# The main part of a Fourier and gated two-layer kernel in 31 chunks instead of 34, with fourth-stage units that may lie across two chunks

## The chip, the cores and the metric

The kernel runs on one core of a Trainium2 chip. Its metric is the device time of one execution in microseconds; the smaller, the better. Engines are named as in the profile: PE (matrix products, with PEld for its weight loads), DVE, ACT and POOL (elementwise work), SP (issues transfers).

## The reference, cut to what matters

```python
X = np.fft.rfft(x, axis=1)                    # x: 8 x 3008 x 256
F = (filt_r + 1j * filt_i)[None, :, :]
y = np.fft.irfft(X * F, n=3008, axis=1)       # 24064 tokens of 256
h = y.reshape(24064, 256) @ w_in              # 256 x 2048
g = h * np.cos(h)
out = g @ w_out                               # 2048 x 256
```

All of it is fp32. The kernel splits each operand of a product into a high and a low part and makes three matmuls of one product (high with high, low with high, high with low).

## The kernel before

The transform is computed as matrix products in four stages, one batch of 3008 tokens after the other. Stage 1 (L351 to L361) makes one matmul of 96 x 512 at L357, which DVE copies out of PSUM at L359. Stages 2 and 3 (L364 to L415) are made of triples of matmuls of 512 columns at L280 to L282. Behind a stage-2 triple DVE multiplies by the filter in six instructions: four at L398, one at L399, one at L400, and the last of them frees the PSUM buffer. ACT frees that of stage 3 by the copy at L413. Stage 4 (L521 to L581) works in units of 235 tokens: a load, four or eight short matmuls of 120 columns at L547, a copy of ACT at L572, two operations of DVE at L573 and L574, and the split into a high part (ACT, L577) and a low part (POOL, L578), which land in the y tiles of a chunk. All four stages share two PSUM buffers, which the program calls ps.

The y tiles feed the main part, which takes the first 15604 tokens in 34 chunks: 32 of 470 tokens and two of 282. A chunk has eight steps. In each, `hidden` (L676) makes 12 matmuls of the chunk's width into one of two PSUM buffers called hp (L684). `gate` (L692) then goes over twice the width in each instruction: ACT rounds (L694), DVE subtracts (L695), ACT takes the sine (L698), DVE multiplies (L699) and with this frees hp, ACT casts to gh (L704), POOL makes the remainder gl (L705). Two steps later, `project` (L709) makes 12 matmuls (L719) of gh and gl into the two accumulators acc0 and acc1, of which there is one each. After the eighth step ACT copies each of them into a tile o (L731), which frees it for the next chunk, and issues the store (L732). The tiles o come from a pool of their own with two buffers. Each chunk's tokens are two whole stage-4 units, so that a unit never crosses a chunk's end. After the main part a tail, which is not touched, takes the other 8460 tokens in wide blocks.

Work of the transform is planned into the main part's steps by a table of due times (`plan` and `run_due`, L977 to L998); the step at which the fourth-stage unit of a chunk falls due is counted back from that chunk's begin (`BEFORE4`, `EACH4`). The list scheduler of the framework then sets each engine's order. An engine works its queue in that order; the numbers behind names, as in hp_9813, are the program's own running numbers and differ between the two programs.

Of the kernel before, what the change touches and what calls it, by code (L numbers as in the profile page):

```python
# [10 lines left out]
F32 = mybir.dt.float32  # L11
# [8 lines left out]
NK = 24  # L20
# [17 lines left out]
BEFORE4, EACH4 = 68, 12  # L38
SMALL, FAST = 4, 34
HALF = 252  # L40
# [137 lines left out]
def fft_filter_then_cos_glu(ctx: ExitStack, tc: tile.TileContext, ins, outT):  # L178
# [29 lines left out]
    def load_mats(*names):  # L208
        for i, name in enumerate(names):
# [6 lines left out]
            m = const.tile([rows, 2 * cols], F32R, name=name)  # L216
# [3 lines left out]
    def load_full(*names):  # L220
        for name in names:
            mats[name] = const.tile(list(ins[name].shape), F32, name=name)
            nc.sync.dma_start(mats[name], ins[name])
# [7 lines left out]
    chunks = _chunks()  # L231
    RUN = 5 * TJ
    token0 = chunks[FAST][0] * TJ
# [224 lines left out]
    z2c = dram.tile([4, chunks[0][1], n23 - DIRECT, 2 * D], F32, name="z2c", bufs=1)  # L458
# [11 lines left out]
    def first23(i, fas, fbs):  # L470
# [38 lines left out]
        if i < n23 - DIRECT:  # L509
            nc.sync.dma_start(z2c.rearrange("e g i c -> (e g) i c")[:, i], z[: 4 * chunks[0][1]])  # L510
# [11 lines left out]
    def stage4(c, half):  # L522


        j0, n = chunks[c]
        r, w = n * NK, n * Q
        rows = z2.rearrange("j q d -> (j q) d")[j0 * 2 * Q + half * w :][:w]
        zf = fft.tile([P, 2, D], F32, name="z4", tag="ld", bufs=5)[:r]
        if c == 0:
            zf = zf[: 10 * (n23 - DIRECT)]  # L530
            of = z2c[2 * half : 2 * half + 2].rearrange("a g i (k d) -> (g i k) a d", k=2)
# [634 lines left out]
```

## Time and profile before

| | us |
|---|---|
| median of three runs | 2420.87 |
| fastest and slowest run | 2420.4, 2420.91 |
| profiled execution | 2419.05 |
| its span | 2417.2 |
| PE busy | 2386.4 |
| POOL busy | 1822.7 |
| ACT busy | 1672.6 |
| DVE busy | 1647.6 |

The profiled execution lasts 1.85 us longer than its span, and it is 1.82 us faster than the median. Busy time of PE is the union of its matmuls' spans; a matmul's span reaches into the next one's, so the interval from start to start is what one costs in a row.

### The profile page before, as it was taken

What the parts mean: (1) busy time and instruction counts of PE and PEld (TensorE: products, weight loads), DVE (VectorE), ACT (ScalarE), POOL (GpSimd) and SP (SyncE); (2) the same over time, 40 slices, a digit from 0 to 9 for tenths busy, and PEclk for the clock granted to TensorE, in tenths of its full rate; (3) what the DMA queues carried; (4) which work ended last, traced back from release to release, by engine and by line L of the source; (5) the groups of instructions that cost most, each with busy time, mean ns of one, the idle gap of its engine ahead of it and who ended that gap; (6) DMA issues with size and microseconds to landing.
All of it is one profiled execution on the core that took longest, in us unless ns stands there. A gap on an engine that the chain in (4) does not pass through costs nothing.

```text
span 2417.2 us, 36437 instructions
## 1 busy us (share of the span) xinstructions
PE 2386.4 (99%) x12703; PEld 2091.1 (87%) x12703; DVE 1647.6 (68%) x2376; ACT 1672.6 (69%) x2521; POOL 1822.7 (75%) x1463
## 2 busy tenths in 40 slices
PE   7999999999999999999999999999999999999999
PEld 2788998888888888888888888888999999999998
DVE  5846756675576667667666766765777777777776
ACT  4876677667677766766776676666767677676776
POOL 3886678878697877879787887965777777777775
PEclk9999999999999999999999999999999999999999
DMA  8844354534464454445555453541000000000000
GB/s 294 251 158 131 126 141 129 185 127 133 127 199 151 136 185 140 140 140 172 157 145 173 142 151 102 187 148 48 22 22 30 22 26 26 22 26 26 22 14 18
DMA packets 188303, 277.62 MB, mean 115 GB/s; under 512 B 19440, under 2 KB 103344, under 8 KB 188120
## 3 DMA queue, kind: packets, MB, share of 16 engines
q1 hardware_dynamic: 155448, 223.11, 30.7%
q10 hardware_dynamic: 32672, 52.18, 6.0%
q8 instruction: 101, 1.65, 0.3%
q14 instruction: 82, 0.67, 0.1%
HBM read 177.16 MB, written 98.06 MB: 114 GB/s over the span
## 4 chain that ended last, share of the span: by engine, by line
PE 95%; DMA 2%; DVE 1%; ACT 0%; POOL 0%; SPq 0%; issue 0%; ACTq 0%; POOLq 0%; DVEq 0%
PE hp L684 28%; PE acc L719 28%; PE acc L849 15%; PE x L765 8%; PE w L765 4%; PE ps L547 4%; PE ps L765 2%; PE ps L357 2%; PE ps L280 2%; PE ps L281 2%; PE ps L282 2%; DMA zf<-z1f 1%; PE ps L330 0%; DMA xf<-in_x 0%; DMA raw<-in_w_out 0%; DMA ff<-in_fb 0%
## 5 line engine op out<-in xcount | busy, mean ns | idle before, releaser
L705 POOL TENSOR_TENSOR gl<-g,gh 128x940 fp32r<-128x940 f32 (+1 forms) x264 | 574.8, 2178 | 242.4 <-ACT gh L704 155.7
L684 PE MATMUL hp<-y,w_in 128*128 128x470 f32 (+1 forms) x3264 | 751.8, 373 | 5.3 <-DVE g L699 4.6
L684 PEld LDWEIGHTS hp<-y,w_in 128*128 128x128 f32 x3264 | 604.6, 189 | 92.2 <-issue 5.7
L719 PE MATMUL acc<-gh,w_out 128*128 128x470 f32 (+1 forms) x2176 | 608.6, 373 | 0.0
L719 PEld LDWEIGHTS acc<-gh,w_out 128*128 128x128 f32 x2176 | 404.5, 189 | 58.0 <-issue 1.7
L695 DVE TENSOR_TENSOR g<-g,hp 128x940 f32<-128x940 int32 (+1 forms) x272 | 301.3, 1108 | 187.9 <-ACT g L694 181.7
L699 DVE TENSOR_TENSOR g<-g,hp 128x940 f32<-128x940 f32 (+1 forms) x272 | 301.5, 1108 | 165.4 <-ACT g L698 163.2
L698 ACT ACTIVATE g<-g,half_pi 128x940 f32<-128x940 f32 (+1 forms) x272 | 289.8, 1065 | 136.7 <-DVE g L695 134.1
L719 PE MATMUL acc<-gl,w_out 128*128 128x470 f32 (+1 forms) x1088 | 373.1, 375 | 0.8 <-POOL gl L705 0.8
L704 ACT CAST gh<-g 128x940 fp32r<-128x940 f32 (+1 forms) x272 | 260.7, 958 | 116.4 <-DVE g L699 108.6
L694 ACT ACTIVATE g<-hp 128x940 int32<-128x940 f32 (+1 forms) x272 | 254.5, 936 | 114.4 <-PE hp L684 111.0
L352 POOL TENSOR_TENSOR xh<-xf,xh 48x512 fp32r<-48x512 f32 x192 | 245.5, 1291 | 34.2 <-ACT xh L351 23.2
L747 ACT ACTIVATE qg<-qg,half_pi 128x496 f32<-128x496 f32 (+1 forms) x272 | 188.2, 712 | 77.4 <-DVE qg L746 77.4
L719 PEld LDWEIGHTS acc<-gl,w_out 128*128 128x128 f32 x1088 | 204.2, 188 | 30.4 <-POOL gl L705 1.4
L359 DVE COPY z1t<-ps 96x512 f32<-96x512 f32 x192 | 130.5, 685 | 113.3 <-PE ps L357 111.2
L398 DVE SCALAR_TENSOR_TENSOR sw<-ps,sg,f 64x256 f32<-64x256 f32 x336 | 162.5, 483 | 51.0 <-PE ps L282 46.0
L849 PE MATMUL acc<-hg,w_out 128*128 128x496 f32 (+1 forms) x548 | 185.0, 392 | 0.0
L849 PE MATMUL acc<-hgh,w_out 128*128 128x496 f32 (+1 forms) x544 | 183.5, 391 | 0.6 <-POOL hgh L827 0.6
L849 PE MATMUL acc<-hgl,w_out 128*128 128x496 f32 (+1 forms) x540 | 182.4, 392 | 0.0
L351 ACT CAST xh<-xf 96x512 fp32r<-96x512 f32 x192 | 114.3, 616 | 26.8 <-PE ps L357 26.1
L404 POOL TENSOR_TENSOR yl<-ya,yh 128x512 fp32r<-128x512 f32 x84 | 108.9, 1298 | 27.2 <-ACT yh L403 19.5
L771 ACT COPY sum<-x 128x496 f32<-128x496 f32 (+1 forms) x136 | 78.5, 577 | 58.6 <-PE x L765 58.2
(163 smaller groups left out, 4190.1 us busy)
## 6 DMA issues: line engine op xcount, KB each, us to landing
xf<-in_x SPq DMA_DIRECT2D x224, 192.0 KB
z<-z1t SPq DMA_DIRECT2D x192, 192.0 KB
z<-z SPq DMA_DIRECT2D x98, 240.0 KB
f<-in_fb SPq DMA_DIRECT2D x84, 256.0 KB
f<-in_fa SPq DMA_DIRECT2D x84, 256.0 KB
zf<-z SPq DMA_DIRECT2D x84, 256.0 KB
z<-z2t ACTq DMA_DIRECT2D x84, 256.0 KB
zg<-z SPq DMA_DIRECT2D x72, 256.0 KB
```

The lines of the kernel that those rows point to most:

```text
L352: nc.gpsimd.tensor_tensor(xh[:Q], xf[:Q, v], xh[:Q].bitcast(F32), ALU.subtract)
L684: mm = nc.tensor.matmul(hp[:, u, :nt], w_in[s][w][:, t, fs], y[:, t, :nt], start=(t == 0 and n == 0), stop=(t == NDT - 1 and n == 2))
L694: rounded = nc.scalar.activation(g.bitcast(I32), h, AF.Copy, bias=0.25)
L695: rest = nc.vector.tensor_tensor(g, g.bitcast(I32), h, ALU.subtract)
L698: sine = nc.scalar.activation(g, g, AF.Sin, bias=half_pi, scale=-TWO_PI)
L699: mult = nc.vector.tensor_tensor(g, g, h, ALU.mult)
L704: cast = nc.scalar.copy(gh, g)
L705: lower = engine.tensor_tensor(gl, g, gh.bitcast(F32), ALU.subtract)
L719: nc.tensor.matmul(acc, w_out[s][w][:, u, es], g[:, u], start=(s == 0 and u == 0 and n == 0), stop=(s == NFT // 2 - 1 and u == 1 and n == 2))
L747: nc.scalar.activation(g, g, AF.Sin, bias=half_pi, scale=-TWO_PI)
L765: nc.tensor.matmul(bank[:, p * n : (p + 1) * n], ws[a], y[b], start=first and p == i == 0, stop=last and i == 2, skip_group_check=True)
L849: nc.tensor.matmul(acc, w[a][:, u, e * P : (e + 1) * P], b[:, :, p], start=(q, u, p, n) == (0, 1, 0, 0), stop=(end and p == 1 and n == 2))
```

## The change

The main part takes the same 15604 tokens in 31 chunks: four of 470, one of 464 and 26 of 510 tokens. The stage-4 units keep their size, and 26 of them now lie across the begin of a chunk: such a unit goes to a tile y4s (one buffer), its split is made in two pieces, and the second piece is written when the next chunk has begun (`LATE4`). Its due times count from the begin of the chunk before (`APART4`, `EACH4`). The y tiles and the gate tiles are now laid out for 512 tokens, at multiples of 64 bytes in each row; before, a second half began at 1880 bytes. To make room, the pool of the o tiles is gone, and every o takes a buffer of a ring of five ("ld") that the transform's loaded tiles and their first sums use (zf, z4); and the constants of the start and of the main part share buffers. The diff, cut:

```diff
-BEFORE4, EACH4 = 68, 12
-SMALL, FAST = 4, 34
-HALF = 252
+HALF, WIDE = 252, 512
+SIZES = [470] * 4 + [464] + [510] * 26
+APART4, EACH4, LATE4 = 22, 10, 3
...
+def _units():
+    pairs = [5] * 8 + [3] * 4 + [5] * ((2 * B * NJ - 52) // 5)
+    starts = np.concatenate([[0], np.cumsum(pairs)])
+    return [(int(a), int(c), int(a) * NA) for a, c in zip(starts, pairs)]
...
-            m = const.tile([rows, 2 * cols], F32R, name=name)
+            m = const.tile([P, 2 * cols], F32R, name=name, tag=name)[:rows]
...
-        if c not in ys:
-            ys[c] = [ypool.tile([P, NDT, 5 * TJ], F32R, name=f"y{i}") for i in range(2)]
-        y = fft.tile([P, 2 * HALF], F32, name="y4", bufs=1)[:, : NDT * 5 * NA]...
+            parts = [(k, max(t0, begins[k]), min(t0 + size, begins[k + 1])) for k in range(len(SIZES)) if ...]
+            if len(parts) > 1:
+                flat = outs_pool.tile([P, NDT, 5 * NA], F32, name="y4s")
+            else:
+                flat = fft.tile([P, 512], F32, name="y4", bufs=1)[:, : NDT * 5 * NA]...
...
-        cast = nc.scalar.copy(yh, y)
-        sub = (nc.vector if c < 2 else nc.gpsimd).tensor_tensor(yl, y, yh.bitcast(F32), ALU.subtract)
+        for i, (k, a, b) in enumerate(parts):
+            if i:
+                yield
+            if k not in ys:
+                ys[k] = [ypool.tile([P, 1024], F32R, name=f"y{i}").rearrange("p (t n) -> p t n", t=NDT) for i in range(2)]
+            yh, yl = (v[:, :, a - begins[k] : b - begins[k]] for v in ys[k])
+            of = flat[:, :, a - t0 : b - t0]
+            cast = nc.scalar.copy(yh, of)
+            sub = (nc.vector if u < 4 else nc.gpsimd).tensor_tensor(yl, of, yh.bitcast(F32), ALU.subtract)
...
-        g = moe.tile([P, 2, HALF * 2], F32, name="g")[:, :, :nt]
+        g = moe.tile([P, 2, WIDE], F32, name="g")[:, :, :nt]
...
-                if stages:
-                    o = fft.tile([P, 512], F32, name="o", tag="ld", bufs=5)[:, :nt]
-                else:
-                    o = opool.tile([P, RUN], F32, name="o")[:, :nt]
+                o = fft.tile([P, 512], F32, name="o", tag="ld", bufs=5)[:, :nt]
...
+                at = [slot(begins[k - 1]) + 2 + (t0 - first) * APART4 / (5 * NA) + t * EACH4 for t in range(NDT)]
+            ready = lambda k=k, ready=ready: ready() and now_at[0] >= k - 1
+            if t0 + n * NA > begins[k + 1]:
+                due.append([slot(begins[k]) + LATE4, False, g, lambda k=k: now_at[0] >= k])
```

The lines of the kernel move by 6 to 18: L684 is L702 after the change, L694 to L705 are L712 to L723, L719 is L737, L731 is L746, L547 is L555, L573 and L574 are L581 and L582, L357 and L359 are L363 and L365, L280 to L282 are L286 to L288, L398 to L400 are L404 to L406.

The order of the queues moves with it, as the two programs show at three places. They are counted here by chunk from 0, and a row names line, kind, what it writes, what it reads and its shape.

The first place is in the transform's stage 2, late in the program (chunk 24 after the change). DVE before, at the 62nd stage-2 group:

```order
L398 SCALAR_TENSOR_TENSOR sw_12770<-ps_12766,sg_79,f_12561 64x256 x4
L573 TENSOR_TENSOR y4_12863<-ps_12793,odd_12864 128x10x24
L399 TENSOR_TENSOR ps_12766<-ps_12766,f_12561 128x512
L574 TENSOR_TENSOR y4_12863<-ps_12793,odd_12864 128x10x23
L400 TENSOR_TENSOR ya_12771<-ps_12766,sw_12770 128x512
L695 TENSOR_TENSOR g_12905<-g_12905,hp_12870 128x2x470
L699 TENSOR_TENSOR g_12905<-g_12905,hp_12870 128x2x470
L398 SCALAR_TENSOR_TENSOR sw_12837<-ps_12833,sg_79,f_12612 64x256 x4
L695 TENSOR_TENSOR g_12969<-g_12969,hp_12944 128x2x470
```

DVE after the change, at the 62nd and 63rd group:

```order
L404 SCALAR_TENSOR_TENSOR sw_12119<-ps_12115,sg_79,f_11947 64x256 x4
L404 SCALAR_TENSOR_TENSOR sw_12185<-ps_12181,sg_79,f_11993 64x256 x4
L713 TENSOR_TENSOR g_12350<-g_12350,hp_12330 128x2x510
L405 TENSOR_TENSOR ps_12115<-ps_12115,f_11947 128x512
L405 TENSOR_TENSOR ps_12181<-ps_12181,f_11993 128x512
L713 TENSOR_TENSOR g_12426<-g_12426,hp_12406 128x2x510
L406 TENSOR_TENSOR ya_12120<-ps_12115,sw_12119 128x512
L717 TENSOR_TENSOR g_12350<-g_12350,hp_12330 128x2x510
L406 TENSOR_TENSOR ya_12186<-ps_12181,sw_12185 128x512
```

The six instructions of a group stood together before; now the eight L404 of two groups stand first, and two gate operations stand ahead of the L406 that frees ps_12115. On PE, the last matmul into ps_12115 is followed by one triple of 512 columns and the 12 matmuls of hp_12406, and then by this:

```order
L702 MATMUL hp_12406<-y1_11746,w_in0_3_86 128x510
L702 MATMUL hp_12406<-y0_11745,w_in1_3_87 128x510
L555 MATMUL ps_12219<-m40_617,z4_12163 128x120
L555 MATMUL ps_12219<-m41_619,z4_12163 128x120
L555 MATMUL ps_12219<-m40_617,z4_12163 128x120
L555 MATMUL ps_12219<-m41_619,z4_12163 128x120
L702 MATMUL hp_12484<-y0_11745,w_in0_4_88 128x510
L702 MATMUL hp_12484<-y1_11746,w_in0_4_88 128x510
```

The four L555 write ps_12219, which takes the buffer of ps_12115; hp_12484 takes that of hp_12330. Where DVE had eight L398 in a row before (in chunk 22), 41 matmuls of 470 columns and one of 512 stood on PE between the group's last matmul and the next use of its buffer.

The second place is the begin of chunk 19, with stage 1 of a later batch beside it. PE before, around the 121st stage-1 matmul, and after, at the 124th and 125th:

```order
L684 MATMUL hp_10334<-y0_9894,w_in0_1_82 128x470
L357 MATMUL ps_10212<-xh_10138,m1_1513 96x512
L684 MATMUL hp_10334<-y1_9895,w_in0_1_82 128x470
L684 MATMUL hp_10334<-y0_9894,w_in1_1_83 128x470
L719 MATMUL acc0_9989<-gh_10252,w_out0_7_110 128x470
L719 MATMUL acc0_9989<-gh_10252,w_out1_7_111 128x470
L357 MATMUL ps_10233<-xh_10141,m1_1513 96x512
L719 MATMUL acc1_9990<-gh_10252,w_out0_7_110 128x470
```

```order
L702 MATMUL hp_9813<-y0_9299,w_in1_1_83 128x510
L363 MATMUL ps_9820<-xh_9732,m1_1506 96x512
L702 MATMUL hp_9813<-y0_9299,w_in0_1_82 128x510
L702 MATMUL hp_9813<-y1_9300,w_in0_1_82 128x510
L702 MATMUL hp_9813<-y0_9299,w_in1_1_83 128x510
L363 MATMUL ps_9843<-xh_9735,m1_1506 96x512
L702 MATMUL hp_9872<-y0_9299,w_in0_2_84 128x510
L702 MATMUL hp_9872<-y1_9300,w_in0_2_84 128x510
```

Before, a projection (acc) followed the hidden step; now three hidden steps, hp_9756, hp_9813 and hp_9872, follow each other, the third in the buffer of the first. DVE before, at the 124th stage-1 copy, and after:

```order
L359 COPY z1t_10293<-ps_10291 96x512
L359 COPY z1t_10325<-ps_10323 96x512
L695 TENSOR_TENSOR g_10459<-g_10459,hp_10446 128x2x470
L699 TENSOR_TENSOR g_10459<-g_10459,hp_10446 128x2x470
L359 COPY z1t_10369<-ps_10367 96x512
L359 COPY z1t_10383<-ps_10381 96x512
L695 TENSOR_TENSOR g_10514<-g_10514,hp_10496 128x2x470
L699 TENSOR_TENSOR g_10514<-g_10514,hp_10496 128x2x470
```

```order
L365 COPY z1t_9807<-ps_9805 96x512
L713 TENSOR_TENSOR g_9778<-g_9778,hp_9756 128x2x510
L365 COPY z1t_9822<-ps_9820 96x512
L365 COPY z1t_9845<-ps_9843 96x512
L717 TENSOR_TENSOR g_9778<-g_9778,hp_9756 128x2x510
L713 TENSOR_TENSOR g_9831<-g_9831,hp_9813 128x2x510
L717 TENSOR_TENSOR g_9831<-g_9831,hp_9813 128x2x510
```

Before, the two gate operations of a step followed each other; now two copies of stage 1 stand between L713 and L717 of hp_9756, the second of them of the matmul that stands right ahead of hp_9872 on PE.

The third place is chunk 11, steps 2 to 6. DVE before, at the 59th stage-1 copy, and after, at the same:

```order
L359 COPY z1t_6060<-ps_6058 96x512
L695 TENSOR_TENSOR g_6256<-g_6256,hp_6243 128x2x470
L359 COPY z1t_6095<-ps_6093 96x512
L699 TENSOR_TENSOR g_6256<-g_6256,hp_6243 128x2x470
L359 COPY z1t_6124<-ps_6122 96x512
L695 TENSOR_TENSOR g_6304<-g_6304,hp_6286 128x2x470
L359 COPY z1t_6148<-ps_6146 96x512
L699 TENSOR_TENSOR g_6304<-g_6304,hp_6286 128x2x470
```

```order
L365 COPY z1t_5716<-ps_5714 96x512
L365 COPY z1t_5742<-ps_5740 96x512
L713 TENSOR_TENSOR g_5929<-g_5929,hp_5916 128x2x510
L365 COPY z1t_5766<-ps_5764 96x512
L365 COPY z1t_5792<-ps_5790 96x512
L713 TENSOR_TENSOR g_5980<-g_5980,hp_5967 128x2x510
L717 TENSOR_TENSOR g_5929<-g_5929,hp_5916 128x2x510
L365 COPY z1t_5836<-ps_5834 96x512
```

Before, L699 of a step followed its L695 with one copy between; now four copies and the L713 of the next step stand ahead of the L717 that frees hp_5916. On PE, the hidden steps hp_5916, hp_5967, hp_6022, hp_6084 and hp_6146 follow each other with no projection between them: the tiles o of chunk 10 take the ring buffers of two z4 tiles, one of which is read by the matmuls L555 that stand behind hp_5967.

## Rows read from the trace of the kernel before

**Rows 1.** The page: busy time of each engine, then the chain that ended last.

```profile
PE 2386.4 (99%) x12703; PEld 2091.1 (87%) x12703; DVE 1647.6 (68%) x2376; ACT 1672.6 (69%) x2521; POOL 1822.7 (75%) x1463
...
PE 95%; DMA 2%; DVE 1%; ACT 0%; POOL 0%; SPq 0%; issue 0%; ACTq 0%; POOLq 0%; DVEq 0%
PE hp L684 28%; PE acc L719 28%; PE acc L849 15%; PE x L765 8%; PE w L765 4%; PE ps L547 4%; PE ps L765 2%; PE ps L357 2%; PE ps L280 2%; PE ps L281 2%; PE ps L282 2%; DMA zf<-z1f 1%; PE ps L330 0%; DMA xf<-in_x 0%; DMA raw<-in_w_out 0%; DMA ff<-in_fb 0%
```

**Rows 2.** Windows: stretch, its length, each engine's busy us and instructions, clock, DMA share.

```profile
1000.00:1200.00 200.00, 200.00 (x960) 174.75 (x960) 135.19 (x181) 138.20 (x185) 163.04 (x106) 1.00 0.51 155
```

**Rows 3.** Waits of PE between 100 and 1660 us: total, times, longest.

```profile
PE hp L684 <- DVE g L699: 1.1, 2, 0.6
PE ps L357 <- ACT z2t L413: 0.6, 1, 0.6
```

**Rows 4.** Timeline of PE: start, length, work; 470-token matmuls back to back.

```profile
1649.17 2.73 PE L684 MATMUL hp<-y,w_in 128*128 128x470 f32 x12
1651.74 1.02 PE L719 MATMUL acc<-gh,w_out 128*128 128x470 f32 x4
...
1659.44 1.05 PE L547 MATMUL ps<-m,z 120*128 120x120 f32 x8
```

**Rows 5.** Timeline of PE in a chunk of 282 tokens.

```profile
306.14 3.29 PE L684 MATMUL hp<-y,w_in 128*128 128x282 f32 x24
309.27 0.69 PE L719 MATMUL acc<-gh,w_out 128*128 128x282 f32 x4
```

**Rows 6.** Timeline of PE: two triples of 512 columns and what starts after each.

```profile
689.25 0.39 PE L280 MATMUL ps<-zh,m 128*128 128x512 f32 x1
...
689.94 2.09 PE L684 MATMUL hp<-y,w_in 128*128 128x470 f32 x9
...
697.71 0.39 PE L280 MATMUL ps<-yh,m 128*128 128x512 f32 x1
...
698.40 0.38 PE L719 MATMUL acc<-gl,w_out 128*128 128x470 f32 x1
```

**Rows 7.** Lines by form: gate operations and the copy out of PSUM.

```profile
L705 POOL TENSOR_TENSOR gl<-g,gh 128x940 fp32r<-128x940 f32 x248 | 552.4, 2228 | 226.4 <-ACT gh L704 145.7 <-issue 50.1 <-DMA xf<-in_x 11.3
L699 DVE TENSOR_TENSOR g<-g,hp 128x940 f32<-128x940 f32 x256 | 289.7, 1132 | 158.5 <-ACT g L698 156.3
L695 DVE TENSOR_TENSOR g<-g,hp 128x940 f32<-128x940 int32 x256 | 289.5, 1131 | 178.4 <-ACT g L694 172.4 <-POOL zf L383 1.4 <-POOL yl L404 1.1
L698 ACT ACTIVATE g<-g,half_pi 128x940 f32<-128x940 f32 x256 | 277.5, 1084 | 134.2 <-DVE g L695 131.6 <-ACT o L731 0.9 <-DVE y L573 0.4
L694 ACT ACTIVATE g<-hp 128x940 int32<-128x940 f32 x256 | 244.3, 954 | 105.7 <-PE hp L684 103.2 <-POOL xh L352 0.8
L359 DVE COPY z1t<-ps 96x512 f32<-96x512 f32 x192 | 130.5, 685 | 113.3 <-PE ps L357 111.2 <-DMA out_t<-o 1.2
```

**Rows 8.** Timeline of DVE where two stage-2 groups stand together.

```profile
1095.31 3.98 DVE L398 SCALAR_TENSOR_TENSOR sw<-ps,sg,f 64x256 f32<-64x256 f32 x8
1099.22 0.68 DVE L399 TENSOR_TENSOR ps<-ps,f 128x512 f32<-128x512 f32 x1
1099.93 1.14 DVE L695 TENSOR_TENSOR g<-g,hp 128x940 f32<-128x940 int32 x1
1100.98 0.69 DVE L399 TENSOR_TENSOR ps<-ps,f 128x512 f32<-128x512 f32 x1
1101.59 1.28 DVE L400 TENSOR_TENSOR ya<-ps,sw 128x512 f32<-128x512 f32 x2
```

**Rows 9.** Timeline of PE at the same place.

```profile
1094.87 0.39 PE L282 MATMUL ps<-zl,m 128*128 128x512 f32 x1
...
1104.09 1.05 PE L547 MATMUL ps<-m,z 120*128 120x120 f32 x8
```

**Rows 10.** Timeline of PE where two stage-1 matmuls stand before a hidden step.

```profile
1205.84 0.62 PE L357 MATMUL ps<-xh,m 96*96 96x512 f32 x2
1206.86 2.79 PE L684 MATMUL hp<-y,w_in 128*128 128x470 f32 x12 [0.41 <-DVE g L699]
```

More of the change, by code (lines that the diff above doesn't have):

```diff
@@ L221, in load_full @@
         for name in names:
-            mats[name] = const.tile(list(ins[name].shape), F32, name=name)
+            rows, cols = ins[name].shape
+            shared = {"f1": "m1", "f2": "m2", "f3": "m3", "f30": "m30"}.get(name)
+            mats[name] = const.tile([P, 2 * cols if shared and rows == P else cols], F32, name=name, tag=shared or name)[:rows, :cols]
             nc.sync.dma_start(mats[name], ins[name])
@@ L229, in fft_filter_then_cos_glu @@
     w_out = [[const.tile([P, 2, D], F32R, name=f"w_out{i}_{s}") for i in range(2)] for s in range(NS)]
-    chunks = _chunks()
+    units = _units()
+    begins = [0]
+    for size in SIZES:
+        begins.append(begins[-1] + size)
     RUN = 5 * TJ
-    token0 = chunks[FAST][0] * TJ
+    token0 = begins[-1]
+    MAIN = [a for _, _, a in units].index(token0)
     wide = _wide(B * S - token0)
@@ L709, in project @@
     def project(c, s):
-        nt = chunks[c][1] * TJ
+        nt = SIZES[c]
         if s == 0:
@@ L969, in fft_filter_then_cos_glu @@
         load_full("m40", "m41")
-    steps = [(c, s) for c in range(FAST) for s in range(NS)]
+    steps = [(c, s) for c in range(len(SIZES)) for s in range(NS)]
     due = []
@@ L1030, in fft_filter_then_cos_glu @@
     for k, (t, m) in enumerate(wide):
-        need = {(FAST + u // 2, u % 2) for u in range(2 * (len(chunks) - FAST)) if u * RUN // 2 < t + 2 * m}
-        at = [slot(chunks[FAST][0]) + SLOTS * NS * k - a for a in AHEAD_BLOCK]
+        need = {MAIN + u for u in range(len(units) - MAIN) if u * RUN // 2 < t + 2 * m}
+        at = [slot(token0) + SLOTS * NS * k - a for a in AHEAD_BLOCK]
         ready = lambda need=need: need <= done
@@ L1054, in fft_filter_then_cos_glu @@
         c, s = steps[k]
+        now_at[0] = c
         if k < len(steps):
@@ L1066, in fft_filter_then_cos_glu @@
             parts.append(project(*steps[k - LAG]))
-        rate = chunks[c][1] / 5
-        now = slot(chunks[c][0]) + SLOTS * rate * s
+        rate = SIZES[c] / RUN
+        now = slot(begins[c]) + SLOTS * rate * s
         for g in parts:
@@ L1079, in fft_filter_then_cos_glu @@
     with tc.manual_schedule(engines={mybir.EngineType.PE}):
-        now = slot(chunks[FAST][0])
+        now = slot(token0)
         begin(0, 0)
```

130 lines of the change are left out of this document (66 added, 64 removed).

## The prediction

> **What bounds the kernel now.** I read the page first: PE is busy for 2386.4 of 2417.2 us, and the chain that ended last runs over PE for 95% of the span, 28% at L684 and 28% at L719, the two lines that the change makes fewer of [rows 1]. Then the windows: in the main part PE is busy for 200.00 of 200 us at a granted clock of 1.00, the 2.4 GHz level, while DVE, ACT and POOL work for 135, 138 and 163 us [rows 2]. So there is no idle PE time to win here, and only two things can move the end: the price of the matmuls, and new waits of PE. The waits of PE between 100 and 1660 us come to 1.7 us, in three places [rows 3]. A matmul's result is there 0.39 us after its start, some 0.16 us after the next could start, so each of the three cost about 0.16 us more than it shows: 2 us in all.
>
> **Part 1: fewer, wider matmuls.** The main part had 32 x 192 = 6144 matmuls of 470 columns and 2 x 192 = 384 of 282. It will have 26 x 192 = 4992 of 510, 768 of 470 and 192 of 464: 576 fewer, over the same columns. The prices are intervals from start to start. Of 470: 48 in 1659.44 - 1649.17 = 10.27 us, 214 ns [rows 4]. Of 282: 24 in 3.13 us, 130 ns [rows 5]. Of 510 there is no row. Its neighbours are two triples of 512 at 0.69 us, 230 ns each [rows 6]. From 470 upwards, 40 columns at 2.4 GHz are 16.7 ns more, so 230.7. The line through 282 and 470 is steeper (84 ns over 188 columns) and gives 231.9; the line through 470 and 512 is flatter and gives 229.2. I take 230.6, next to the 512 row, and keep 229.2 and 232 as ends. Before: 6144 x 214 + 384 x 130 = 1364.7 us. After: 4992 x 230.6 + 768 x 214 + 192 x 211.5 = 1356.1 us. **PE saves 8.6 us**, 15.6 at 229.2 and 1.6 at 232.
>
> The Trainium skill, page "TensorE: Matmul & The Clock Gate", section "Wait — 56ns, not 53.3ns?", puts the interval of a warm matmul at N divided by 2.4 GHz and 2.5 ns. By it, 576 fewer would save 576 x 2.5 = 1.4 us and no more. The rows here differ from the page: it would give 198 ns at 470, where the trace has 214.
>
> **Part 2: the alignment.** The second halves of the y and gate tiles move from 1880 to 2048 bytes. In a hidden step and in a projection half of the matmuls read a second half; the 12 of a hidden step take 2.57 us and the 36 behind them 7.70, 214 ns each in both [rows 4], which is on the line from 282 to 512 and leaves nothing for a misaligned half. I put it at nothing, for PE and for the other engines.
>
> **Part 3: the other engines.** A gate instruction grows from 940 to 1020 elements, 8.5%: L694 to 1.03 us, L695 and L699 to 1.23, L698 to 1.18, L705 to 2.42 [rows 7], and there are 24 fewer of each. The 26 split units add 26 casts of ACT and 26 subtractions of POOL, each shorter than a whole one. DVE, ACT and POOL have 37 to 65 us of 200 free [rows 2], so their sum costs nothing. What costs is **where** an instruction stands when PE waits for it. Freeing hp takes the end of the matmul and the four gate operations, 0.16 + 1.03 + 1.23 + 1.18 + 1.23 = 4.8 us. Before, hidden steps and projections alternate, and PE has some 36 other matmuls, 7.7 us, in between. After the change, chunk begins come when the last unit's second piece is late, or when o waits for a ring buffer and so keeps the accumulators; the scheduler then lets hidden steps follow each other. In the order after the change PE has under 4.9 us of work between the end of a hidden step and the one that reuses its buffer at seven places; before at one. I work the tight places out from the queues, with the durations above; 510 counts as 0.23 us.
>
> (a) Chunk 24, DVE at the two stage-2 groups. Counted from the start of the last matmul into ps_12115: its result is there at 0.39. Eight L404 take 3.91 (1095.31 to 1099.22), L713 1.05 x 1.085 = 1.14, two L405 0.71 + 0.61, L713 again 1.14, L406 0.68 [rows 8]: 8.58 us. PE has 16 intervals until L555, 3.68 us: it waits 4.9. Then L717 needs 1.14 more until 9.72, where PE with the four L555 (0.36) would be at 8.94: 0.8. Sum 5.7. At the eight L398 of before the same DVE work was covered, since PE had 9.22 us of matmuls (1094.87 to 1104.09) [rows 9]; if such a cover is there, (a) is nothing, but the order shows 16 rows. Lower end 4.0.
>
> (b) Chunk 11, five hidden steps in a row. With the end of hp_5916 at 0, hp_5967 ends at 3.0, its L712 at 4.2, L713 at 5.4, and only then comes the L717 that frees hp_5916: 6.6. PE would start hp_6022 at 4.05 (12 + 4 intervals and four L555): 2.6. Then hp_6022 to hp_6146 has 3.36 us of work against 4.8: 1.4. Sum 4.0, at least 2.1 by the bare gate chains.
>
> (c) Chunk 19. Five stage-1 matmuls stand nearly together on two PSUM buffers; each round of two needs a matmul and a copy, 0.39 + 0.69 us [rows 7]; I count 1.0 lost. Then hp_9872: one interval before it starts the matmul whose copy stands ahead of L717, so 0.39 + 0.69 + 1.23 = 2.3 against 0.23: 2.0. A milder case is in the trace of before: with two L357 right ahead of a hidden step PE waits 0.41 for L699 [rows 10]. Sum 3.0, at least 2.0.
>
> (d) Chunk 25. Between hp_12762 and hp_12902 PE has 20 intervals, 4.6 us; a stage-2 group that ends at 2.9 puts four L404 (1.96) ahead of L717 (1.23): 6.1, so 1.5. Ahead of that, the late unit y4s and two o stand in ACT's queue in front of what hp_12762 needs; by the queues 0 to 3.5. I take 2.5 in all.
>
> (e) Chunks 4, 12 and 13: a late second piece, and a second o that lies in the same buffer as the first and so waits for its store, whose landing no row gives. Each could cost 0 to 3 us; I take 1.5 in all, near the lower end, because most waits of before on such places were short.
>
> Sum 5.7 + 4.0 + 3.0 + 2.5 + 1.5 = **16.7 us** of new waits, 9.6 with the lower ends, some 24 with the upper. The 2 us of before's own tight places go, since the order there is another.
>
> **Sum.** -8.6 + 16.7 - 2 = +6.1 us. The profiled execution of 2419.05 (span and 1.85) becomes 2425.2; it lies 1.82 under the median, so the median of 2420.87 becomes **2427.0**.
>
> **Rivals.** *The gate chain is shorter than its scaled rows.* If a release takes 4.1 instead of 4.8 us, (b) and (d) fall to about 1.0 together and (c) to 0.5, (e) to nothing, (a) to its lower end of 4.0: 5.5. Then -8.6 + 5.5 - 2 = -5.1, 2415.8, and at the flat price of 229.2 ns 2409: **faster**. It decides once the waits stay under some 5.8 us at 8.6 saved, or under 12.8 at 15.6. For it speaks that DVE starts an instruction some 0.09 us before the one ahead of it has ended (1099.93 and 1.14 against 1100.98 [rows 8]), so that a chain of means is too long; against it, that (a) hardly depends on the gates. Chance 0.20, at 2414.
>
> *The lower ends hold.* -8.6 + 9.6 - 2 = -1: 2420, and up to 2425.7 with waits of 15. No change that can be measured. Chance 0.32, at 2422.
>
> *A matmul costs by its columns.* 282 columns take 0.461 ns each, 470 0.455, 512 0.449: nearly the same. At 232 ns for 510 the saving is 1.6, and the waits remain: -1.6 + 16.7 - 2 = +13.1, 2434. Chance 0.12. The rule of the Trainium skill's page "TensorE: Matmul & The Clock Gate" (section "Wait — 56ns, not 53.3ns?"), with its 1.4 us, would give 2434 too.
>
> *The change does not do what it says:* should the tiles' new alignment be what decides, every main matmul would change its price; the rows above speak against it, and I leave it inside the ends of the price.
>
> **How the numbers follow.** A measurement of this kernel can tell 0.2%, 4.8 us, from no change: same means 2416.0 to 2425.7. The forecast (2425.7 to 2431) has 0.36 and the dear matmul 0.12: slower 0.48. Same has 0.32, faster 0.20. As the faster and the slower side hold two thirds of it between them, the range must reach both: the forecast's own range is 2422 to 2432, and to leave out no more than 2 in 10 I go from 2412 to 2437.
>
> **What would show it.** At 510 columns, 24 matmuls in a row would take 5.5 us (5.57 at 232). The waits of PE in the main part would name DVE's L717 and L406 with over 10 us in all, the longest of them near 5 us at an L555 of ps at some three quarters of the main part, and hidden steps of chunks 11, 19 and 25 waiting one to three. I am wrong if those waits stay under 5 us, if PE is busy without a break there, or if the interval at 510 lies outside 229 to 232. The tail should move as a whole.

## The result and the profile after the change

The change makes the kernel slower: 2435.39 us, median of four runs (2433.64 to 2438.74), against 2420.89 us of the kernel before. The ratio is 1.0062, with an interval of 1.0044 to 1.0079: 14.5 us in the medians. A later set of four runs gave 2436.28 us against 2420.02, a ratio of 1.0065 (1.0051 to 1.0079). The forecast was 2427.0, slower by 6.1, with a range from 2412 to 2437.

The profiled execution lasts 2438.74 us, its span 2436.9: 19.7 us more than the span of before. It is the longest of the four runs, and the profiled execution of before lay 1.82 us under its median, so the two traces lie further apart than the medians do.

The page of the kernel after, busy time and the chain that ended last; its lines answer to [rows 1].

```profile
PE 2394.6 (98%) x12127; PEld 2005.5 (82%) x12127; DVE 1636.5 (67%) x2328; ACT 1661.8 (68%) x2469; POOL 1822.6 (75%) x1465
...
PE 89%; POOL 3%; DMA 2%; DVE 2%; issue 2%; ACT 1%; SPq 0%; POOLq 0%; ACTq 0%; DVEq 0%
```

PE has 576 matmuls fewer and is busy for 8.2 us longer. The chain runs over PE for 89% of the span where it was 95%, and POOL has come into it with 3%. So PE now waits for others, and some of its matmuls have become slower.

Windows of 200 us, in the columns of [rows 2] (stretch, length, busy us and count of PE, PEld, DVE, ACT, POOL; granted clock; DMA share; GB/s):

```profile
1200.00:1400.00 200.00, 191.69 (x845) 153.85 (x844) 125.66 (x166) 130.00 (x172) 152.33 (x102) 0.98 0.50 153
1400.00:1600.00 200.00, 200.00 (x900) 162.50 (x899) 130.29 (x164) 138.71 (x181) 163.05 (x107) 1.00 0.45 140
```

The second of these stretches looks like [rows 2]: PE busy without a break at a clock of 1.00. The first has 8.3 us of idle PE time, **and in the same stretch** the granted clock is 0.98. So it is from 600 to 800 and from 1000 to 1200 us, with PE busy for 195.66 and 197.48 us at a clock of 0.99.

The waits of PE from 100 to 1660 us (total, times, longest), which answer to [rows 3]:

```profile
PE hp L702 <- DVE g L717: 5.9, 5, 2.0
PE ps L555 <- DVE ya L406: 5.1, 1, 5.1
PE ps L286 <- ACT z2t L419: 1.9, 2, 1.3
PE acc L737 <- POOL gl L723: 1.0, 2, 0.6
PE ps L555 <- DVE z1t L365: 0.5, 1, 0.5
PE ps L286 <- DVE y4s L582: 0.4, 1, 0.4
PE ps L363 <- DVE z1t L365: 0.4, 2, 0.2
PE acc L737 <- ACT gh L722: 0.2, 1, 0.2
```

These are 15 waits, 15.5 us as shown one by one, against 1.7 us in three before. With the 0.16 us per wait that the view does not show they cost 17.9 us, against 2.2.

The timeline of PE (start, length, work, and in brackets the idle time ahead with what ended it) at the longest wait, in chunk 24:

```profile
1325.08 2.96 PE L702 MATMUL hp<-y,w_in 128*128 128x510 f32 x12
1327.87 0.40 PE L288 MATMUL ps<-zl,m 128*128 128x512 f32 x1
...
1329.82 3.03 PE L702 MATMUL hp<-y,w_in 128*128 128x510 f32 x12 [0.86 <-DVE g L717]
1337.92 2.06 PE L555 MATMUL ps<-m,z 120*128 120x120 f32 x8 [5.07 <-DVE ya L406]
1339.64 5.16 PE L702 MATMUL hp<-y,w_in 128*128 128x510 f32 x12
1344.64 0.62 PE L737 MATMUL acc<-gh,w_out 128*128 128x510 f32 x2
```

Ahead of the wait 12 matmuls of 510 columns take 1327.87 - 1325.08 = 2.79 us. Behind it the same 12 take 1344.64 - 1339.64 = 5.00 us. Windows of 4 us over the same place:

```profile
1334.00:1338.00 4.00, 0.08 (x1) 0.09 (x1) 4.00 (x6) 2.44 (x3) 4.00 (x4) 0.94 0.34 107
1338.00:1342.00 4.00, 4.00 (x14) 3.53 (x15) 3.52 (x5) 3.12 (x6) 3.35 (x3) 0.50 0.93 291
1342.00:1346.00 4.00, 4.00 (x14) 3.22 (x13) 0.04 (x1) 1.61 (x2) 3.04 (x3) 0.71 0.55 192
```

The granted clock fell to 0.50, the 1.2 GHz level, at the end of the wait, and came back between 1342 and 1346. **The wait was paid twice:** 5.1 us of standing still, and then matmuls of 417 ns each in place of 232. The two next longest waits show the same. In chunk 11 the 12 matmuls behind the wait take 649.05 - 644.68 = 4.37 us, and the clock from 640 to 650 us is 0.83; in chunk 19 the span of such a 12 is 4.58 us where 2.96 is usual, and the clock from 1060 to 1070 us is 0.89.

```profile
644.68 4.54 PE L702 MATMUL hp<-y,w_in 128*128 128x510 f32 x12 [1.55 <-DVE g L717]
649.05 0.40 PE L363 MATMUL ps<-xh,m 96*96 96x512 f32 x1
...
1067.19 4.58 PE L702 MATMUL hp<-y,w_in 128*128 128x510 f32 x12 [2.00 <-DVE g L717]
```

Of the main part, 13.6 us passed at the lower level (3.4, 3.4 and 6.8 at the three places). Half of that, less what PE stood still in it, is lost: I count 6.2 us, over the intervals from start to start in these stretches against the mean of the same shape elsewhere.

Where the 19.7 us come from, by the two traces. The main part, from the first to the last hidden step, grew from 1604.1 to 1621.8 us, 17.7: waits 17.9 - 2.2 = +15.7, lower clock behind waits +6.2, lower clock at the main part's start +0.7 (last section), matmuls -5.3; these make 17.3, 0.4 less than measured. The tail, from the last hidden step to the end of the last matmul, grew from 740.5 to 742.5 us, 2.0.

### The profile page after: what moved, and what is told of

The parts are those of the page before. It is cut to its first block, busy times and chain, and to the rows that moved or that the text cites. A ratio compares the mean times of both kernels' runs of the same rounds, so it can differ in the third digit from the quotient of the medians.

```text
span 2436.9 us, 35124 instructions
## 1 busy us (share of the span) xinstructions
PE 2394.6 (98%) x12127; PEld 2005.5 (82%) x12127; DVE 1636.5 (67%) x2328; ACT 1661.8 (68%) x2469; POOL 1822.6 (75%) x1465
## 4 chain that ended last, share of the span: by engine, by line
PE 89%; POOL 3%; DMA 2%; DVE 2%; issue 2%; ACT 1%; SPq 0%; POOLq 0%; ACTq 0%; DVEq 0%
PE hp L702 26%; PE acc L737 25%; PE acc L864 15%; PE x L780 8%; PE w L780 4%; PE ps L555 4%; PE ps L780 2%; PE ps L363 2%; PE ps L286 1%; PE ps L287 1%; PE ps L288 1%; POOL gl L723 1%; POOL zf L389 1%; POOL zl L394 1%; DMA ff<-in_fa 1%
## 5 line engine op out<-in xcount | busy, mean ns | idle before, releaser
L702 PE MATMUL hp<-y,w_in 128*128 128x510 f32 (+2 forms) x2976 | 752.8, 394 | 10.2 <-DVE g L717 9.5
L723 POOL TENSOR_TENSOR gl<-g,gh 128x1020 fp32r<-128x1020 f32 (+2 forms) x240 | 570.6, 2378 | 233.6 <-ACT gh L722 163.8
L702 PEld LDWEIGHTS hp<-y,w_in 128*128 128x128 f32 x2976 | 561.4, 190 | 139.4 <-issue 10.4
L737 PE MATMUL acc<-gh,w_out 128*128 128x510 f32 (+2 forms) x1984 | 595.6, 392 | 0.2 <-ACT gh L722 0.2
L737 PEld LDWEIGHTS acc<-gh,w_out 128*128 128x128 f32 x1984 | 371.1, 188 | 83.2 <-issue 2.5
L713 DVE TENSOR_TENSOR g<-g,hp 128x1020 f32<-128x1020 int32 (+2 forms) x248 | 297.8, 1201 | 184.3 <-ACT g L712 181.4
L717 DVE TENSOR_TENSOR g<-g,hp 128x1020 f32<-128x1020 f32 (+2 forms) x248 | 297.8, 1201 | 162.5 <-ACT g L716 161.3
L716 ACT ACTIVATE g<-g,half_pi 128x1020 f32<-128x1020 f32 (+2 forms) x248 | 282.6, 1139 | 138.0 <-DVE g L713 132.5
L737 PE MATMUL acc<-gl,w_out 128*128 128x510 f32 (+2 forms) x992 | 362.0, 393 | 1.7 <-POOL gl L723 1.7
L712 ACT ACTIVATE g<-hp 128x1020 int32<-128x1020 f32 (+2 forms) x248 | 250.4, 1010 | 127.0 <-PE hp L702 117.5
L722 ACT CAST gh<-g 128x1020 fp32r<-128x1020 f32 (+2 forms) x248 | 256.7, 1035 | 117.7 <-DVE g L717 110.0
L737 PEld LDWEIGHTS acc<-gl,w_out 128*128 128x128 f32 x992 | 186.1, 188 | 44.2 <-POOL gl L723 2.8
L404 DVE SCALAR_TENSOR_TENSOR sw<-ps,sg,f 64x256 f32<-64x256 f32 x336 | 162.4, 483 | 77.3 <-PE ps L288 72.3
L365 DVE COPY z1t<-ps 96x512 f32<-96x512 f32 x192 | 130.4, 685 | 109.6 <-PE ps L363 108.6
L357 ACT CAST xh<-xf 96x512 fp32r<-96x512 f32 x192 | 114.0, 616 | 31.6 <-PE ps L363 30.6
L555 PEld LDWEIGHTS ps<-m,z 120*128 120x128 f32 (+1 forms) x816 | 111.3, 193 | 15.6 <-DVE ya L406 5.5
```

What stands on the lines that cost most here:

```text
L702: mm = nc.tensor.matmul(hp[:, u, :nt], w_in[s][w][:, t, fs], y[:, t, :nt], start=(t == 0 and n == 0), stop=(t == NDT - 1 and n == 2))
L712: rounded = nc.scalar.activation(g.bitcast(I32), h, AF.Copy, bias=0.25)
L713: rest = nc.vector.tensor_tensor(g, g.bitcast(I32), h, ALU.subtract)
L716: sine = nc.scalar.activation(g, g, AF.Sin, bias=half_pi, scale=-TWO_PI)
L717: mult = nc.vector.tensor_tensor(g, g, h, ALU.mult)
L722: cast = nc.scalar.copy(gh, g)
```

## The experiments

### One group later

The changed kernel with the stage-2 group that collides in chunk 24 due eight units later.

```diff
             t = start + step * (ones + 2 * i + 2) + GAP12
+            t += 8 if (b, i) == (6, 2) else 0
```

> The changed kernel, with one stage-2 group of the seventh batch (number 2) due 8 slots later. The queues are the same up to chunk 24; there the eight L404 no longer stand in a row. If the wait of 5.07 us at L555 and the 6.8 us at half clock behind it are the largest single loss, the time falls by 5.7 (waits) and some 3.4 (clock), from 2435.4 to about 2426, no wait over 2.5 us is left and the clock stays at 1.00 near 1340 us. If waits cost only their own length, about 2430. If the width or the layout of the tiles is what costs, about 2435.

Measured: 2427.63 us against 2420.16, ratio 1.0028 (1.0018 to 1.0039). The profiled execution took 2425.14. DVE's timeline at the place of the long wait:

```profile
1325.06 1.98 DVE L404 SCALAR_TENSOR_TENSOR sw<-ps,sg,f 64x256 f32<-64x256 f32 x4
...
1329.12 0.68 DVE L406 TENSOR_TENSOR ya<-ps,sw 128x512 f32<-128x512 f32 x1
```

Here four L404 stand together, and the group's L406 ends 4.7 us after its first L404. In the kernel after, eight stand together and the first L406 ends 8.2 us after the first of them:

```profile
1329.71 3.98 DVE L404 SCALAR_TENSOR_TENSOR sw<-ps,sg,f 64x256 f32<-64x256 f32 x8
...
1337.18 0.68 DVE L406 TENSOR_TENSOR ya<-ps,sw 128x512 f32<-128x512 f32 x1
```

Between these two rows DVE works without a gap through L713, two L405 and L713. So two groups that are served together, with gate operations between their parts, are what made the longest wait. Taking them apart left 7.5 us of the 14.5, each against the kernel before of its own set: it gave back 7.0. In the trace the waits fell from 15 with 15.5 us to 12 with 9.0, which is 7.0 us with the hidden 0.16 of each: 5.07 and 0.86 in chunk 24 are gone, and in chunk 25 0.65 and 0.45, where 0.44 came. No stretch at the lower clock is left in the main part behind its start; the two profiled executions, 13.6 us apart, differ by that clock's 6.2 too. The medians alone, between the 2426 expected with the clock and the 2430 without, do not show how much the clock gave back.

### Old widths in the new layout

The changed kernel with the widths of before; rings, tile layout and due times as changed, and again two whole units in a chunk.

```diff
-SIZES = [470] * 4 + [464] + [510] * 26
+SIZES = [470] * 4 + [282] * 2 + [470] * 28
```

> The changed kernel with the chunk sizes of before (32 of 470, two of 282), so that no unit lies across two chunks; the layout at 64 bytes, the ring for o and the new due times stay. If the loss comes from split units and the order that they bring, some 2 us more waits than before are left (two of 1.5 to 2 us near chunk 22): 2421 to 2425. If the ring for o, or the layout, is what costs, over 2428. If the layout makes matmuls cheaper, 470 columns take 213 ns instead of 214 and the time is 2415 to 2419.

Measured: 2426.0 us against 2420.16, ratio 1.0023 (1.0014 to 1.0033), somewhat above what was expected. Without one wide chunk and without one split unit the kernel is 5.8 us slower than before. The waits of PE in the main part:

```profile
PE hp L702 <- DVE g L717: 1.8, 2, 1.5
PE ps L286 <- ACT z2t L419: 1.7, 1, 1.7
PE acc L737 <- ACT o L746: 1.0, 2, 0.6
PE ps L555 <- DMA z<-z: 0.8, 2, 0.7
```

5.3 us in seven waits, other ones than in the kernel after. Two of them follow each other at 1113.35 (1.65 us) and 1115.81 (1.49 us), and the twelve matmuls of 470 behind the second take 1120.67 - 1115.81 = 4.86 us in place of 2.57:

```profile
1115.81 5.07 PE L702 MATMUL hp<-y,w_in 128*128 128x470 f32 x12 [1.49 <-DVE g L717]
1120.67 0.63 PE L286 MATMUL ps<-zh,m 128*128 128x512 f32 x1
```

The new tiles moved the price of a matmul by under 1% and not all one way: at full clock 470 columns took 213.6 ns on the mean against 214.2 before, 512 columns 233.1 against 231.4. In sum the main part's matmuls, outside waits, came to 0.8 us less. The tail is 1.1 us longer than before's (741.6 against 740.5).

### The tiles o from another ring

The changed kernel, with o in the ring of five that the weights' preparation uses.

```diff
-                o = fft.tile([P, 512], F32, name="o", tag="ld", bufs=5)[:, :nt]
+                o = wprep.tile([P, 512], F32, name="o", tag="t", bufs=5)[:, :nt]
```

> The changed kernel with o in another ring of five buffers (that of zg), so that no o waits for a z4 or zf tile. If o's ring is the reason for the bunches of hidden steps in chunk 11 and for the place in chunk 24, both go: 10 us less wait, about 2424. If the order is only drawn anew, the bunch of chunk 11 stays with its 4 us, the wait at the eight L404 goes, and others come (chunks 13, 19 and 25, 3 to 5 us each): 2432 to 2442.

Measured: 2440.89 us against 2420.16, ratio 1.0087 (1.0070 to 1.0104). The timeline of PE in chunk 11 and chunk 19:

```profile
643.79 3.03 PE L702 MATMUL hp<-y,w_in 128*128 128x510 f32 x12 [1.55 <-DVE g L717]
...
651.77 3.03 PE L702 MATMUL hp<-y,w_in 128*128 128x510 f32 x12 [1.04 <-DVE g L717]
...
1071.00 4.57 PE L702 MATMUL hp<-y,w_in 128*128 128x510 f32 x12 [3.49 <-DVE g L717]
```

The bunch of hidden steps in chunk 11 stays with its waits of 0.54, 1.55 and 1.04, though no o shares a buffer with a z4 any more. The part ahead of the prediction says that the tiles o take the ring buffers of two z4 tiles there; that is so, but it is not what bunches the steps; what does stays open. Elsewhere the order came out worse. In chunk 11 the clock stayed at 1.00 behind the same 1.55 us.

### The ring alone

The kernel before, 34 chunks and old tiles, with o always from the shared ring.

```diff
-                if stages:
-                    o = fft.tile([P, 512], F32, name="o", tag="ld", bufs=5)[:, :nt]
-                else:
-                    o = opool.tile([P, RUN], F32, name="o")[:, :nt]
+                o = fft.tile([P, 512], F32, name="o", tag="ld", bufs=5)[:, :nt]
...
-    opool = outs.enter_context(tc.tile_pool(name="opool", bufs=2, reuse_waits="tile"))
```

> The kernel before, its chunks of 470 unchanged, with one thing of the change: the output tile o of the gates always comes from the five-buffer ring that it shares with the loads, and its own two-buffer pool is gone. Theory 'the order drawn anew is what costs': the planner prices this ring, so the queues come out in another order and TensorE gets some new waits of 1 to 2 us in the main part, about 4 us in sum; 2424 to 2426, in the neighbourhood of the run with 31 chunks mostly of 470. Rival 'the tiles and the split units cost, the ring nothing': 2420 to 2421.5.

Measured: 2425.42 us against 2420.15, ratio 1.0022 (1.0013 to 1.0031), as the first theory had it. The waits of PE in the main part:

```profile
PE hp L684 <- DVE g L699: 1.6, 2, 1.1
PE ps L280 <- ACT z2t L413: 1.4, 1, 1.4
...
PE acc L719 <- ACT o L728: 0.7, 1, 0.7
```

One change of a ring, which moves no work for PE, costs 5.3 us. By the two traces the main part grew by 5.4: 3.3 of it are waits (five with 4.7 us against three with 1.7), of which 0.7 is for an o and the others are for gates and transform pieces that the new order has brought together; some 1.0 is the lower clock at the main part's start, which changes from one execution to the next (last section); 1.1 lies in intervals without a wait in the view. The sum is close to the 5.8 that all of the new layout cost without its widths, but the two orders are different, so it is not shown that the other parts of the layout cost nothing.

### A wait put into the tail

The kernel before, with one add of the tail done nine times, and in a second kernel four times.

```diff
-            nc.vector.tensor_tensor(v, x, p7, ALU.add)
+            for _ in range(9 if (c, q) == (8, 1) else 1):
+                nc.vector.tensor_tensor(v, x, p7, ALU.add)
```

> The kernel before; in the tail, at the last pass of inverse transforms, one VectorE add of 510 columns (v = x + p7 of pair 8, quad 1) is done nine times in place of once, with the same result. TensorE, which has nothing else queued there, waits some 5 us longer in one place. Theory 'a wait costs itself and then a stretch at the lower clock': about +5.4 for the wait and 1.7 to 3.4 more for matmuls of some 460 ns in place of 230 right behind it; 2427.5 to 2430. Rival 'the clock has nothing to do with waits': the wait alone, 2425.5 to 2426.5, the granted clock 1.00 behind it.

> As the run with nine adds, but with four: TensorE waits some 1.5 to 2.5 us longer in one place. Theory 'a wait of this size may already bring the lower clock, in some executions and not in others': 2421.5 to 2424.5 with a wide spread between runs. Rival 'only long waits bring it': 2421.5 to 2423, narrow, the granted clock 1.00 behind the wait.

Measured with nine: 2428.34 us against 2420.15, ratio 1.0033 (1.0020 to 1.0047), 8.2 us. With four: 2421.58 us, ratio 1.0006 (0.9996 to 1.0015). The timeline of PE with nine adds:

```profile
2047.59 1.64 PE L765 MATMUL x<-y,sum 128*128 128x248 f32 x6 [4.98 <-DVE v L815]
2049.03 1.48 PE L765 MATMUL x<-diff,sum 128*128 128x248 f32 x6
```

and with four:

```profile
2043.80 0.96 PE L765 MATMUL x<-y,sum 128*128 128x248 f32 x6 [0.96 <-DVE v L815]
2044.60 0.84 PE L765 MATMUL x<-diff,sum 128*128 128x248 f32 x6
```

Behind 4.98 us of waiting, six matmuls of 248 columns take 1.44 us; behind 0.96 us the same six take 0.80. Windows of 2 us with nine adds:

```profile
2049.00:2051.00 2.00, 2.00 (x10) 1.92 (x9) 1.25 (x2) 1.73 (x4) 0.00 (x0) 0.53 0.03 8
2051.00:2053.00 2.00, 2.00 (x15) 1.82 (x14) 0.84 (x2) 1.08 (x3) 1.40 (x2) 1.00 0.00 0
```

This is the disputed cost by itself, in a kernel that the change does not touch: a wait of 5 us brings the lower clock, and the clock returns some 3.4 us later. By the rows the wait costs 4.98 + 0.16 and the clock 1.7, 6.8 in all; the tail in this trace is longer by as much (747.2 us against 740.5), and the 8.2 of the medians has an interval wide enough for that (4.8 to 11.4). The second kernel made a shorter wait than the 1.5 to 2.5 us meant, so it says only that 0.96 us left the clock alone here.

### The same kernels once more

The changed kernel and the kernel with one group later were each profiled a second time.

> The changed kernel once more, for a second profiled execution. Theory 'waits are fixed by the order of work, the lower clock comes behind some of them and not always': the same waits within 0.3 us each (5.1 at the fourth-stage unit of chunk 24, 1.3 to 2.0 at the gates of chunks 11 and 19), but other stretches at the lower clock; median 2433 to 2438, and a profiled execution with fewer such stretches is shorter by 1.7 us for each 3.4 us less of them. Rival 'the lower clock belongs to the places': the same four stretches again, the same time.

> The kernel with one stage-2 group eight due units later, once more, for a second profiled execution. Its first profiled execution (2425.14, among the fastest of its eight runs) had the waits of 1.55 us in chunk 11 and 2.00 us in chunk 19 and no lower clock behind either; the changed kernel had the lower clock behind both, in two executions. Theory 'it differs from execution to execution': the same waits within 0.1 us, the lower clock behind one or both of them this time, and 1.7 to 3.4 us more than the first execution, 2426.5 to 2428.5. Rival 'it belongs to the program': clock 1.00 at both places again, 2425 to 2425.5.

The changed kernel took 2436.28 us (2433.4 to 2437.28), its second profiled execution 2437.28. The same waits stood there, but for the 0.86 us in chunk 24, and **the lower clock came again at the same three places**, for as long as before: for this execution the rival of the expectation held. It does not hold for every one. The mean granted clock on record is 0.993 in the two profiled executions and 0.994 to 0.996 in the six others of the two sets. At 0.996 an execution spent 17 to 22 us at the lower level, where the profiled ones have 34 and 35; as every trace here has at least 10.2 us of it up to the main part's start, the 13.7 us of the three places can hardly all be there. Windows of the second execution over the places in chunks 11 and 24:

```profile
640.00:650.00 10.00, 7.90 (x31) 5.84 (x31) 6.72 (x10) 5.41 (x7) 4.66 (x3) 0.83 0.36 104
1336.00:1346.00 10.00, 8.75 (x36) 7.52 (x37) 6.07 (x8) 6.12 (x11) 7.74 (x6) 0.71 0.79 249
```

The kernel with one group later took 2424.94 us. It has the very waits of its first execution (hp for L717: 5.4 us in five, the longest 2.0, in both). In chunk 19 the first execution kept its clock, the second did not. First:

```profile
1060.00:1070.00 10.00, 8.01 (x35) 6.14 (x34) 5.97 (x6) 6.60 (x8) 3.69 (x3) 1.00 0.35 98
```

Second:

```profile
1060.00:1070.00 10.00, 8.01 (x29) 6.08 (x28) 5.80 (x7) 7.16 (x8) 5.72 (x4) 0.83 0.15 42
```

So the fall behind a wait of 2.00 us is not a property of the program alone: the same wait of the same program has it in one execution and not in another. The time expected with it (2426.5 to 2428.5) was missed: the fall cost some 1.6 us, but this execution came to the main part 0.6 us earlier than the first and had the lower clock there for 3.4 us in place of 6.8, which was worth 1.3.

### The collisions spread

The changed kernel with ten due times shifted, chosen so that the collisions spread out.

```diff
+SHIFT = {(1, 3, 6): -12, (1, 3, 9): 5, (1, 5, 4): 16, (1, 5, 8): -12, (1, 5, 9): 16, (2, 1, 3): -16, (2, 3, 4): -8, (2, 6, 2): 8, (2, 7, 8): 8, (4, 5, 0): -16}
...
-            t = start + step * (i - SOON + 1 if b == 1 else 2 * i + 1)
+            t = start + step * (i - SOON + 1 if b == 1 else 2 * i + 1) + SHIFT.get((1, b, i), 0)
...
-            t = start + step * (ones + 2 * i + 2) + GAP12
+            t = start + step * (ones + 2 * i + 2) + GAP12 + SHIFT.get((2, b, i), 0)
...
+        at = [x + SHIFT.get((4, u, 0), 0) for x in at]
```

> The changed kernel with ten small shifts of planned due times (of single pieces of the first, second and fourth stage of eight groups, by 5 to 16 of the planner's units), chosen so that the collisions of the changed kernel spread out: no wait longer than 1.9 us should be left in the main part and some 4 us more of waits in sum than in the kernel before. Theory 'the change's cost is its order of work, its gain the 576 fewer matmuls': minus 5.3 for the matmuls, plus 4.2 for waits, plus 2.0 in the tail as in the changed kernel, 2420 to 2423, and no lower clock in the main part or one stretch of 1.7 us. Rival 'the wide tiles and split units cost of themselves': 2427 and above, as with the one group moved.

Measured: 2422.04 us against 2420.02, ratio 1.0007 (0.9998 to 1.0016), no difference from before that can be told. The waits of PE in the main part:

```profile
PE ps L364 <- DVE z1t L366: 1.6, 1, 1.6
PE ps L287 <- ACT z2t L420: 1.3, 1, 1.3
PE hp L703 <- DVE g L718: 1.1, 3, 0.4
PE acc L738 <- DVE gl L724: 0.7, 1, 0.7
PE ps L287 <- DVE y4s L583: 0.7, 1, 0.7
```

5.4 us in place of 15.5, with all widths, tiles and split units of the change. So some 12 of the change's 14.5 us (14.5 less 2.0) went with the order alone: they are collisions and the lower clock behind them. Of the widths, tiles and split units no cost is shown beyond the tail's 2.0. One lower stretch is left, behind two waits of chunk 11:

```profile
643.30 0.70 PE L364 MATMUL ps<-xh,m 96*96 96x512 f32 x1 [1.56 <-DVE z1t L366]
644.43 5.44 PE L703 MATMUL hp<-y,w_in 128*128 128x510 f32 x12 [0.42 <-DVE g L718]
649.66 1.28 PE L556 MATMUL ps<-m,z 120*128 120x120 f32 x8
```

Twelve matmuls take 5.23 us there, 2.4 more than elsewhere. No kernel that beats the one before came out: the matmuls give back 5.3 us, and the tail (2.0), the remaining waits and this stretch take it.

## Why the direction was right and the size too small

The prediction's sign, its cause and its range held; its sum came out at less than half of what was measured. That the range held is in part luck: 2435.39 lies 1.6 us under its upper end, which was set for dearer matmuls and longer waits and not for what came. By its own steps:

| step | forecast | in the traces |
|---|---|---|
| fewer, wider matmuls | -8.6 | -5.3 |
| (a) chunk 24 | 5.7 | 0.86 + 5.07, and 0.16 each: 6.25 |
| (b) chunk 11 | 4.0 | 0.55 + 1.55 + 1.03: 3.6 |
| (c) chunk 19 | 3.0 | 0.18 + 0.25 + 2.00: 2.9 |
| (d) chunk 25 | 2.5 | 0.65 + 0.45 + 1.29: 2.9 |
| (e) chunks 4, 12, 13 | 1.5 | 0.42 + 0.24 + 0.37 + 0.59: 2.3 |
| waits of before | -2 | -2.2 |
| lower clock behind waits | no term | 6.2 |
| tail | as a whole, 0 | 2.0 |

**The waits** were right: 16.7 forecast, 17.9 measured, each at the chunk where it was looked for. Of (a) the mechanism held: L555 waits for L406. It came out 1.3 us longer at L555 and the L702 ahead (6.25 against 4.9), because DVE was still at the former step's L717 when the eight L404 could start (1329.71, while PE's last matmul into that buffer began at 1327.87). The second wait that (a) foresaw, 0.8 us for L717, did not come: the trace has eight L555 there and not four, and behind the first wait PE ran at half its clock, so they took 1.72 us where 0.36 was counted, and the gate was done by then. In (c) the stage-1 part was smaller (1.0 forecast, 0.43 seen), and the hidden step's came as forecast (2.0 and 2.00). In (d) the place was right and the mechanism was not: no hidden step waits there, but a projection for gl (0.65), a triple for the late unit y4s (0.45) and another for ACT's copy z2t (1.29). Of (e) only the places held: its waits are for a gate, gh, gl and z2t, and none is for an o. That (d) and (e) came out near their sums is luck. Moving the group of (a) and spreading the others took the waits and the time away together, which shows them as the cause and not only as company.

**The step that failed** is the sum's assumption that every matmul costs its interval at 2.4 GHz. The trace of before has no such fall behind its three short waits [rows 3], [rows 2] showed 1.00, and I gave the clock no term. In the kernel after it fell at the three places with the longest waits and cost 6.2 us in the profiled execution; the kernel with nine adds shows the same without the change. The Trainium skill, page "TensorE: Matmul & The Clock Gate", section "HAM oscillation — how this bites in real kernels", says that idle gaps of PE that are long enough bring it back to the lower clock, so that what follows runs cold. The trace agrees, with 417 ns for a matmul of 510 columns behind the 5.07 us and 232 ahead of it. Weighing that rule against (a) would have added a term for the clock there. By the traces, which are later than the prediction, a fall behind a wait of 5 us cost 1.7 (nine adds) to 3.1 us (chunk 24).

The medians hold less of this than the trace. Against the kernel before of their own set they grew by 14.5 and 16.3 us, 8.4 and 10.2 more than the 6.1 forecast. The matmuls (3.3), the waits (1.0) and the tail (2.0) make 6.3 of that, which leaves 2 to 4 us for the clock; the profiled execution was the longest of its four and had the lowest granted clock of them.

**The price of the matmul** was mis-sized: 230.6 ns was taken for 510 columns, and the trace has 231.7 as the mean over some 4900 intervals at full clock. The two triples of [rows 6] were quick ones: over all triples of before, 476 intervals of 512 columns, the mean is 231.4. The prices of 470 (214.2 against 214) and 282 (131 against 130) were right. With these the main matmuls cost 1366.4 us before and 1360.8 after: 5.6 by the prices, 5.3 over the stretch up to the tail. So width and tiles together buy about 9 ns for each of the 576 that fell away; 0.8 us of it came with the new tiles alone in the kernel with the old widths, where Part 2 put nothing. The step "I take 230.6" should have read more than two rows. The rival that a matmul costs by its columns had 232 and a saving of 1.6; the truth lies between. By the Trainium skill, page "TensorE: Matmul & The Clock Gate", section "Wait — 56ns, not 53.3ns?", an estimate from its 2.5 ns for each matmul has 576 x 2.5 = 1.4 us saved; the measured 5.3 decides against it here.

**The tail** did not move as a whole. The 36 projections of the last chunk that lie in it are now of 510 columns (36 x 17.5 = 0.6 us), and 960 matmuls of two times 248 columns take 226 ns in place of 225 in every trace with wide tiles (1.0 us). What makes these 1 ns dearer was not tried, and the rest of the 2.0 is not accounted for.

**The rivals.** That the gate chain is shorter than its rows fell: the waits came out as the chain of rows said. That the lower ends hold fell with it. That the change does not do what it says fell too: the matmuls are fewer and the split units are there.

**What stays open:** which waits bring the lower clock. Behind 5 us it came in all three traces that have such a wait, behind 1.55 us in chunk 11 twice in the kernel after and in none of three executions of two variants with the same waits, behind 2.00 us in chunk 19 in three of four. A wait of 1.4 to 1.5 us near the tail's start stands in all eleven traces, at 1709.04 us in the kernel after, and the clock stayed at 1.00 behind it every time. And the ring alone costs 5.3 us, mostly through the order: why the scheduler's order gets worse with it was seen only by its outcome.

## What to carry to other kernels

Where one engine is busy without a break, a change of its instructions' size is worth their price difference only; price them by a mean over many intervals, not by two rows. What such a change does to the order of the other engines is the larger term: go through the queues for places where the last instruction that frees a buffer stands behind another's work, and price each wait there once as standing time and once more for the slower matmuls that may follow. A change of one buffer ring can redraw the whole order, so after it the due times should be set anew before its worth is judged.

## What the hardware showed that was not expected

A wait of PE of one and a half to five microseconds, in a stretch that is otherwise full, can bring the granted clock from 1.00 to 0.50 for 3.4 or 6.8 us, which cost another 1.5 to 3.1 us. In the kernel with the other ring it also came behind two shorter waits, 0.67 and 1.08 us, that stand 2 us apart in chunk 25. The same wait has it in one execution and not in the next.

The start of the main part has the lower clock for 3.4 us in four of the eleven traces and for 6.8 in the others, with the main part of before too. Windows from 76 to 88 us, first in the profiled execution of before, then in the kernel with four adds, whose main part and its three waits are those of before:

```profile
76.00:88.00 12.00, 8.41 (x32) 7.16 (x32) 10.49 (x10) 10.79 (x16) 11.15 (x10) 0.86 0.95 312
```

```profile
76.00:88.00 12.00, 8.42 (x26) 6.86 (x25) 8.54 (x10) 10.10 (x15) 11.00 (x10) 0.72 1.02 336
```

The first 48 matmuls of hidden steps took 23.6 us in the first and 24.9 in the second, the main part 1604.1 and 1605.6. In the kernel after, which has the lower clock for 6.8 us too but stood still for part of it, the same 48 took 24.3. So 0.7 of the 19.7 us between the two traces is a matter of the execution and not of the change, and the short start may be most of the 1.82 us by which the profiled execution of before lay under its median; the other executions of before in that set have no trace.
